# Two small transfers made one, and 68 stores issued by another engine, in an attention and two-layer kernel

## The chip, the cores and the metric

The kernel runs on one core of a Trainium2 chip. A core has TensorE (PE, matmuls into PSUM), VectorE (DVE), ScalarE (ACT), GpSimd (POOL) and SyncE (SP, which here only issues DMA transfers and transposes), each working through its own list of instructions in order. Sixteen DMA engines move the data. The metric is the time on the device in microseconds for one execution.

## The reference

Attention with a learned decay over 4 batches, 8 heads, 576 positions and 64 dimensions, then two feed-forward layers over the 2304 tokens:

```python
cum = np.cumsum(np.log(np.clip(f, 1e-4, 1)), axis=-1)
scores = q @ k.T / sqrt(64) + cum[:, :, :, None] - cum[:, :, None, :]   # causal
x = softmax(scores) @ v                     # -> [2304, 512]
x = leaky_relu(x @ w_in, 0.01) @ w_out      # 512 -> 2048 -> 512
h = x @ w_in2                               # 512 -> 1024
solu = h * softmax(h)
y = ((solu - mean) / sqrt(var + 1e-6) * g_ln) @ w_out2
```

## The kernel before

**Stages.** The 32 heads are worked in 16 pairs. For each pair the rows are cut into blocks of 128, and two passes go over them: pass A does blocks 0 and 1 ("full", `prep_full`), pass B does blocks 2 to 4 (`prep_split`, which splits q and k into a high and a low part). Scores are taken on TensorE, the softmax on VectorE and ScalarE, a DMA transpose (`pt<-hl`) turns the probabilities, TensorE multiplies by v, and the sum is put together in an SBUF tile `xr` (L739, L742). At the end of `pair` the tile is stored to DRAM (`xs_d`, L798), from where `load_x` brings it back, by blocks of 256 tokens, as the first layer's input x, and splits it into a high and a low part. The first layer (`ffn_a`) does 9 of the 16 chunks of the hidden layer for each of 9 token blocks and stores its partial sum y to DRAM (`yp_d`, L908; 4 stores of 128 KB for each block, from tiles that the trace calls `yo` or, in their first home, `sd`). The other 7 chunks and the second layer (`ffn_b`, `layer2`) follow when attention is done, from about 470 us on.

**The decay.** `decay` computes the cumulative sums once and stores them to DRAM as `dr_d`, four rows for each head. `prep_full` appends those rows to the tile of q and k of the two heads as contraction rows 64 to 67: for pairs 4 to 15, each of two heads and each of two column ranges (256 wide) had a transfer of its own. Pairs 0 to 3 have their decay in another way (`qa`).

**Weights.** A weight chunk (512 KB) is loaded to a stage tile (`wst`, three of them, early on), unpacked and split by ScalarE, VectorE and GpSimd (L812, L427, L434, L442). The stage is loaded anew when its last reader is done. The x tiles of the first layer are given out only after all operations on the early stages (`main` in the code), as they lie in the same space.

**Order.** Nothing is issued in the order of the program text. Each operation is put down with an engine (or several to choose from), a cost in nanoseconds, a priority and its dependencies; a planner (`P.run`) plays the whole kernel through when it is built, lets each free engine take its most urgent ready operation, and so writes the order of every engine. On the chip each engine then follows its own list and waits on semaphores. A transfer is put down by `move`, whose costs are 475 ns on SyncE and 1,040 ns on GpSimd; the transfer's bytes occupy one model of the DMA engines. A change of an engine or of a cost can therefore move everything behind it. A store on an engine stands in that engine's list until the data that it stores are there.

```python
QUEUES = ("SP",)
d = {SP: 475.0, ACT: 490.0, POOL: 1040.0}
return flex(engs, [d[e] for e in engs], lambda e: queue[e].dma_start(dst(), src()), prio, dma=nbytes / 360.0, **kw)
```

All transfers were issued by SyncE, since `engs` is `QUEUES` where nothing else is said.

Of the kernel before, what the change touches and what calls it, by code (L numbers as in the profile page):

```python
# [47 lines left out]
LD = 51.31  # L48
# [9 lines left out]
TB = 256  # L58
# [4 lines left out]
KB = CQ + 256  # L63
# [286 lines left out]
def mmr(n):  # L350
    return n / 2.4 + 2.5 if n > 255 else 80.0
# [6 lines left out]
def body(tc, kqa, kq, vt, f, wa, w2i, w2o, gln, out):  # L358
# [3 lines left out]
    PE, ACT, DVE, POOL, SP, CTL = "PE", "ACT", "DVE", "POOL", "SP", "CTL"  # L362
# [6 lines left out]
    def tiles(pool, name, n, shape, dt):  # L369
        return [pool.tile(shape, dt, name=f"{name}{i}") for i in range(n)]  # L370
# [10 lines left out]
    xs_d = tiles(dram, "xs_d", B, [128, KD, S], F32)  # L381
    yp_d = tiles(dram, "yp_d", NB, [128, KD, TB], F32)
    dr_d = dram.tile([2 * NP, 4, KQ], F32, name="dr_d")
# [60 lines left out]
    def flex(engs, durs, emit, prio, **kw):  # L444
        box = []
        o = P.op(tuple(engs) if len(engs) > 1 else engs[0], tuple(durs) if len(engs) > 1 else durs[0],
                 lambda: emit(box[0].eng), prio, **kw)
        box.append(o)
        return o

    def copy_f(o, i, n, prio, engs=(ACT, DVE, POOL), scale=None, psum=False, **kw):
        p = 0 if scale is None else 1
        d = {ACT: act(n, p, psum), DVE: (dve(n) if psum else dve2(n)) + 60 * p, POOL: pool1(n) + 84 * p}
        return flex(engs, [d[e] for e in engs], lambda e: copy_on(e, o(), i(), scale and scale()), prio, **kw)
# [7 lines left out]
    def move(dst, src, nbytes, prio, engs=QUEUES, **kw):  # L462
        d = {SP: 475.0, ACT: 490.0, POOL: 1040.0}
        return flex(engs, [d[e] for e in engs], lambda e: queue[e].dma_start(dst(), src()), prio, dma=nbytes / 360.0, **kw)

    def load(buf, dst, src, nbytes, prio, mode="w", **kw):
        return move(dst, src, nbytes, prio, **{mode: [buf]}, **kw)
# [30 lines left out]
    def row(h, p):  # L498

        return KD * h + p if p < KD else 2 * KD + (NP - KD) * h + p - KD  # L500
# [57 lines left out]
    st, QK, VT, U, QA = {}, {}, {}, {}, {}  # L558
# [7 lines left out]
    def prep_full(p, prio):  # L566


        if p < KD:
            bq = QA[0]  # L570
            QK[p] = [[(bq, p), (bq, "n"), (bq, "c")]] * 2, lambda hd: qa[0:66, hd, p], {0: 256, 1: 384}
            return
        bq = P.buf("raw")
        a = lambda r0, r1: bq.t[r0:r1, 0:1024].rearrange("r (h c) -> r h c", h=2)
        load((bq, 0), lambda: a(0, 64), lambda: kqa[p].rearrange("(h d) c -> d h c", h=2), 64 * 1024 * 4, prio - LD)
        for hd in range(2):
            for c0, k0 in ((0, 0), (256, KB)):
                load((bq, (hd, c0)), lambda hd=hd, c0=c0: a(64, 68)[:, hd, c0:c0 + 256], lambda hd=hd, k0=k0: dr_d[row(hd, p), :, k0:k0 + 256], 4096, prio - LD,
                     deps=st["cols"])
        QK[p] = [[bq]] * 2, lambda hd: a(0, 68)[:, hd], {0: 256, 1: 384}  # L580

    def prep_split(p, prio):
# [106 lines left out]
    def scores(p, unit, hd, prio, full):  # L689

        sts, parts, n, at = P.buf("st"), [], 0, 0
        for j, i in enumerate(unit):
            W = 128 * (i + 1)
            joint = i < 2 and len(unit) > 1
            if i == 1 and joint:
                at = 128
            else:
                ps, at = P.buf("ps_s"), 0
            view = lambda at=at, W=W, ps=ps: ps.t[:, at:at + W]
            key = (ps, j) if joint else ps  # L700
            P.op(PE, 4 * W / 2.4 if full else 2 * mmr(W), lambda Q=QK[p], i=i, W=W, view=view: qk_mm(
                Q, full, i, view(), hd, 0, W, True, True), prio, r=QK[p][0][hd], heat=HEAT if full else 1.0,
                **({"rw": [ps]} if at else {"w": [ps]}))
            parts.append([view, sts, j, W, [(n, n + W, 0, W)], key, i])
            n += 2 * W
        for view, _, j, W, _, key, i in parts:
            P.op(DVE, dve(W) + 130, lambda i=i, j=j, view=view: nc.vector.tensor_tensor_reduce(  # L707
                view(), view(), mask[:, 512 - 128 * i:640], -0.125, 3.0e38, ALU.add, ALU.min, sts.t[:, j:j + 1]),
                prio, w=[(sts, j)], rw=[key])
        parts = [x[:6] for x in parts]  # L710
        pt = softmax(parts, prio)
        return {i: (pt, x[4][0][0] // 128) for i, x in zip(unit, parts)}
# [37 lines left out]
    def pv(p, hd, pts, xr, prio):  # L750
        ps, blocks = P.buf("ps_v"), sorted(pts)
        bufs = {id(b): b for b, _ in pts.values()}

        def pe():
            for i in blocks:
                for j in range(i + 1):
                    for k in range(2):
                        mm(ps.t[:, 128 * i:128 * i + 128], vl(p, hd, j), pts[i][0].t[:, pts[i][1] + k * (i + 1) + j, :],
                           j == 0 and k == 0, j == i and k == 1)

        P.op(PE, sum(2 * (i + 1) * mmh(128) for i in blocks), pe, prio, w=[ps], r=[VT[p]] + list(bufs.values()))
        evac(p, hd, ps, xr, 128 * blocks[0], 128 * (blocks[-1] + 1), 128 * blocks[0], prio)

    def pv4(p, pt, xr, prio):
        ps = P.buf("ps_v")

        def pe():
            for hd in range(2):
                o, c = ps.t[:, 64 * hd:64 * hd + 64], slice(64 * hd, 64 * hd + 64)
                for j in range(4):  # L770
                    for k in range(2):
                        mm(o, vl(p, hd, j), pt.t[:, 4 * k + j, c], j == 0 and k == 0, False)
                mm(o, vl(p, hd, 4), pt.t[:, 8, c], False, True)

        P.op(PE, 18 * mmh(64), pe, prio, w=[ps], r=[VT[p], pt])
        for hd in range(2):
            evac(p, hd, ps, xr, 64 * hd, 64 * hd + 64, 512, prio)

    def pair(p, prio, blocks):
        n0 = len(P.ops)  # L780
        b, kd = divmod(p, KD)
        full = len(blocks) == 2
        (prep_full if full else prep_split)(p, prio)
        if 0 in blocks:
            prep_v(p, prio)
        xr = P.buf("xr")
        k = 0
        for hd in range(2):
            pts = {}
            for unit in UNITS[len(blocks)]:  # L790
                pts.update(scores(p, unit, hd, prio + SM + KSTEP * k, full))
                k += 1
            pv(p, hd, pts, xr, prio + AV)
            if hd == HD4 and 4 in blocks:
                pv4(p, scores4(p, prio + SM + KSTEP * k, full), xr, prio + AV)
                k += 1
        c0, c1 = 128 * blocks[0], min(S, 128 * blocks[-1] + 128)
        o = move(lambda: xs_d[b][:, kd, c0:c1], lambda: xr.t[:, c0:c1], 128 * (c1 - c0) * 4, prio - 400, r=[xr])  # L798
        spills.append((b, c0, c1, o))
        attn_ops.extend(P.ops[n0:])  # L800

# [57 lines left out]
    def y_mms(o, c, d, g, n, first, last):  # L859
        w = WO[c].t  # L860
        wh, wl = (w[:, j, 128 * d:128 * d + 128] for j in range(2))
        gh, gl = (g.t[:, j, 0:n] for j in range(2))
        mm(o, wh, gh, first, False)
        mm(o, wh, gl, False, False)
        mm(o, wl, gh, False, last)
# [23 lines left out]
    YPD, FFNB = {}, {}  # L889

    def ffn_a(blk, prio):
        eprio = prio - EP
        xb = load_x(blk, prio, "x")
        gs = [hidden(c, xb, TB, "ps_f", "g", prio + c, eprio + c) for c in range(FA)]
        YPD[blk] = []
        for d in range(KD):
            ps, yo = P.buf("ps_f"), P.buf("yo")
            for q in range(2):
                cs = range(FA // 2 * q, FA if q else FA // 2)

                def pe(cs=cs, d=d, ps=ps):
                    for c in cs:
                        y_mms(ps.t[:, 0:TB], c, d, gs[c], TB, c == 0, c == FA - 1)

                P.op(PE, 3 * len(cs) * mmr(TB), pe, prio + EPD + d, r=[gs[c] for c in cs] + [WO[c] for c in cs],
                     **({"w": [ps]} if q == 0 else {"rw": [ps]}))
            copy_f(lambda yo=yo: yo.t, lambda ps=ps: ps.t[:, 0:TB], TB, eprio + EPD + d, engs=(ACT, DVE), scale=lambda: WSC * WSC, psum=True, w=[yo], r=[ps])
            YPD[blk].append(move(lambda d=d: yp_d[blk][:, d], lambda yo=yo: yo.t, 128 * TB * 4, prio - 3000, r=[yo]))  # L908

    def ffn_b(tb, prio):  # L910
        eprio, blk = prio - 3000, ORDER[tb]
# [233 lines left out]
```

## Time and profile before

| | |
|---|---|
| runs | 849.77, 846.91, 848.83 us; median 848.83 |
| profiled execution | 848.65 us, span 846.9 us from the first to the last instruction |
| granted TensorE clock, mean | 0.993 |
| TensorE busy | 767.9 us (91% of the span) |
| VectorE, ScalarE, GpSimd busy | 519.4, 490.1, 348.8 us |
| DMA | 108.37 MB, all issued through SyncE's queue but for instructions |

Busy time leaves out instructions that only issue a DMA, so SyncE has none, and a GpSimd that issues a store counts as idle. A wait is put down to the operation that came last. The stretch to 90 us is the start (first pairs, weights), 90 to 392 us is attention mixed with the first layer, 392 to 470 us is the first layer alone, and then come the rest and the second layer.

### The profile page before, as it was taken

How to read it: one execution, taken by the hardware profiler on the slowest of the kernel's cores; microseconds unless marked ns; L12 is line 12 of the kernel's file. 1: busy time of each engine (PE TensorE's matmuls, PEld its weight loads, DVE VectorE, ACT ScalarE, POOL GpSimd, SP SyncE). 2: the span in 40 equal slices, each digit the busy share in tenths (PEclk: the TensorE clock that was granted, in tenths of full speed). 3: DMA queues.
4: the chain of work that ended last, by engine and by line, in shares of the span. 5: the costliest groups of instructions: out<-in, count | busy, mean ns of one | idle time of the engine just before them, and what ended most of it. 6: DMA issues, size and time to landing. Idle time of an engine off the chain costs nothing.

```text
span 846.9 us, 16019 instructions
## 1 busy us (share of the span) xinstructions
PE 767.9 (91%) x5648; PEld 695.5 (82%) x5648; DVE 519.4 (61%) x1350; ACT 490.1 (58%) x1242; POOL 348.8 (41%) x448
## 2 busy tenths in 40 slices
PE   1753798979999999999899998999999999999996
PEld 1432698968998999999899987898889988998885
DVE  5788767888888878884654667334633434253551
ACT  4886768889889889884555543232333243333321
POOL 6648545166618564822610443422332233222321
PEclk9999999989999999999999999999999999999999
DMA  8997457687789677694655643321332131312223
GB/s 230 220 223 245 96 130 151 150 221 154 136 162 216 155 163 151 174 160 148 195 172 177 189 104 104 71 79 16 98 71 68 26 87 38 87 26 63 26 56 82
DMA packets 184402, 108.37 MB, mean 128 GB/s; under 512 B 150033, under 2 KB 167137, under 8 KB 184321
## 3 DMA queue, kind: packets, MB, share of 16 engines
q1 hardware_dynamic: 184320, 107.35, 52.3%
q8 instruction: 44, 0.72, 0.4%
q14 instruction: 38, 0.30, 0.1%
HBM read 57.39 MB, written 14.78 MB: 85 GB/s over the span
## 4 chain that ended last, share of the span: by engine, by line
PE 64%; DMA 10%; DVE 9%; ACT 8%; issue 4%; POOL 3%; SPq 0%; ACTq 0%; DVEq 0%; POOLq 0%
PE ps_f L473 40%; PE ph L473 10%; PE py L473 6%; PE ps_s L473 5%; PE ps_v L473 3%; ACT ps_s L657 2%; DMA raw<-w2o 2%; DMA tr<-hl 2%; DMA raw<-kq 2%; DMA wst<-wa 1%; DMA pt<-hl 1%; ACT hl L427 1%; DVE hl L438 1%; DMA qa<-sd 1%; DVE ps_s L707 1%
## 5 line engine op out<-in xcount | busy, mean ns | idle before, releaser
L473 PE MATMUL ps_f<-x,wi 128*128 128x256 f32 x972 | 131.7, 289 | 1.2 <-POOL x L442 1.1
L473 PE MATMUL ps_f<-g,wo 128*128 128x256 f32 x972 | 126.4, 284 | 2.5 <-DVE g L855 2.5
L473 PEld LDWEIGHTS ps_f<-x,wi 128*128 128x128 f32 x972 | 124.7, 193 | 3.1 <-POOL x L442 1.9
L473 PEld LDWEIGHTS ps_f<-g,wo 128*128 128x128 f32 x972 | 120.8, 188 | 4.0 <-DVE g L855 2.9
L473 PE MATMUL ph<-wi,g 128*128 128x512 f32 x408 | 98.5, 397 | 1.4 <-DVE raw L968 1.4
L473 PE MATMUL ps_f<-x,wib 128*128 128x256 f32 x756 | 97.3, 279 | 1.8 <-DVE g L855 1.7
L438 DVE SCALAR_TENSOR_TENSOR hl<-ps_s,st,hl 128x512 f16<-128x512 f32 (+4 forms) x160 | 82.8, 540 | 19.4 <-ACT hl L427 16.5
L473 PEld LDWEIGHTS ps_f<-x,wib 128*128 128x128 f32 x756 | 91.6, 188 | 2.9 <-DVE g L855 2.8
L473 PEld LDWEIGHTS ph<-wi,g 128*128 128x128 f32 x408 | 75.9, 188 | 19.3 <-DVE raw L968 1.6
L855 DVE TENSOR_TENSOR g<-ps_f,g 128x256 fp32r<-128x256 f32 x144 | 60.3, 420 | 48.1 <-ACT ps_f L854 47.2
L853 ACT ACTIVATE g<-ps_f 128x256 fp32r<-128x256 f32 x144 | 54.8, 380 | 59.3 <-PE ps_f L473 58.1
L657 ACT ACTIVATE ps_s<-ps_s,st 128x512 f32<-128x512 f32 (+4 forms) x160 | 78.6, 491 | 10.1 <-DVE st L707 6.1
L473 PE MATMUL ps_f<-wo,x 128*128 128x512 f32 x348 | 84.0, 396 | 0.0
L427 ACT ACTIVATE hl<-ps_s,st 128x512 f16<-128x512 f32 (+4 forms) x151 | 76.1, 532 | 11.6 <-DMA pt<-hl 4.7
L473 PE MATMUL ps_v<-pt,VT 128*128 128x128 f16 (+1 forms) x928 | 62.3, 220 | 20.0 <-DVE xr L742 9.0
L473 PE MATMUL py<-g,wob 128*128 128x256 f32 x567 | 75.6, 278 | 2.0 <-ACT g L427 2.0
L473 PEld LDWEIGHTS ps_f<-wo,x 128*128 128x128 f32 x348 | 64.8, 188 | 15.1
L473 PE MATMUL ps_s<-kq 128*128 128x512 f32 (+5 forms) x256 | 66.7, 380 | 11.6 <-DVE hl L438 5.5
L442 POOL TENSOR_TENSOR kq<-raw,kq 64x576 fp32r<-64x576 f32 (+1 forms) x53 | 67.9, 1283 | 21.5 <-ACT kq L427 15.2
L473 PEld LDWEIGHTS <-VT 128*128 128x128 f16 x928 | 50.0, 102 | 30.4 <-issue 15.4
L473 PEld LDWEIGHTS py<-g,wob 128*128 128x128 f32 x567 | 71.2, 188 | 4.3 <-ACT g L427 2.3
L707 DVE CUSTOM_DVE_ANT_0 ps_s<-ps_s,mask 128x256 f32<-128x256 f32 (+3 forms) x128 | 62.2, 496 | 5.9 <-PE ps_s L473 4.5
(159 smaller groups left out, 1221.7 us busy)
## 6 DMA issues: line engine op xcount, KB each, us to landing
wst<-wa SPq DMA_DIRECT2D x18, 512.0 KB
sd<-xs_d SPq DMA_DIRECT2D x32, 256.0 KB
raw<-kq SPq DMA_DIRECT2D x16, 480.0 KB
raw<-wa SPq DMA_DIRECT2D x14, 512.0 KB
raw<-yp_d SPq DMA_DIRECT2D x18, 256.0 KB
vr<-vt SPq DMA_DIRECT2D x13, 320.0 KB
raw<-w2i SPq DMA_DIRECT2D x8, 512.0 KB
raw<-w2o SPq DMA_DIRECT2D x8, 512.0 KB
```

Of the source, the lines that this page charges most:

```text
L427: nc.scalar.activation(o, i, CP, scale=1.0 if scale is None else scale)
L438: nc.vector.scalar_tensor_tensor(o, a, scale, b, op0=ALU.mult, op1=ALU.subtract)
L442: (nc.vector if eng == DVE else nc.gpsimd).tensor_tensor(o, a, b, op=ALU.subtract)
L473: nc.tensor.matmul(o, lhsT=l, rhs=r, start=start, stop=stop)
L657: P.op(ACT, act(W, 1, True) + 93, lambda view=view, j=j, k=k: nc.scalar.activation(view(), view(), AF.Exp, bias=sts.t[:, j:j + 1], scale=- ...
L707: P.op(DVE, dve(W) + 130, lambda i=i, j=j, view=view: nc.vector.tensor_tensor_reduce(view(), view(), mask[:, 512 - 128 * i:640], -0.125, 3 ...
L853: P.op(ACT, act(n, 0, True), lambda: nc.scalar.activation(g.t[:, 0, 0:n], h(), AF.Prelu, scale=WSC, alpha=0.01), eprio, w=[(g, 0)], r=[ps])
L855: P.op(DVE, dve(n) + 60, lambda: nc.vector.tensor_tensor(g.t[:, 1, 0:n], h(), g.t[:, 0, 0:n].bitcast(F32), op=ALU.subtract), eprio, w=[(g, ...
```

## The change

The two heads' decay rows of one column range are brought by one transfer, so a pair has two of 8 KB instead of four of 4 KB. The store of x at the end of each pair's pass (32 of them) and the stores of the first layer's partial y (36) are issued by GpSimd.

```diff
-        for hd in range(2):
-            for c0, k0 in ((0, 0), (256, KB)):
-                load((bq, (hd, c0)), lambda hd=hd, c0=c0: a(64, 68)[:, hd, c0:c0 + 256], lambda hd=hd, k0=k0: dr_d[row(hd, p), :, k0:k0 + 256], 4096, prio - LD,
-                     deps=st["cols"])
+        for c0, k0 in ((0, 0), (256, KB)):
+            load((bq, c0 + 1), lambda c0=c0: a(64, 68)[:, :, c0:c0 + 256], lambda k0=k0: dr_d[row(0, p):row(1, p) + 1:row(1, p) - row(0, p), :, k0:k0 + 256].rearrange("h r c -> r h c"),
+                 8192, prio - LD, deps=st["cols"])
...
-        o = move(lambda: xs_d[b][:, kd, c0:c1], lambda: xr.t[:, c0:c1], 128 * (c1 - c0) * 4, prio - 400, r=[xr])
+        o = move(lambda: xs_d[b][:, kd, c0:c1], lambda: xr.t[:, c0:c1], 128 * (c1 - c0) * 4, prio - 400, r=[xr], engs=("POOL",))
...
-            YPD[blk].append(move(lambda d=d: yp_d[blk][:, d], lambda yo=yo: yo.t, 128 * TB * 4, prio - 3000, r=[yo]))
+            YPD[blk].append(move(lambda d=d: yp_d[blk][:, d], lambda yo=yo: yo.t, 128 * TB * 4, prio - 3000, r=[yo], engs=("POOL",)))
```

## Rows read from the trace of the kernel before

**Rows 1.** The page: engines' busy time, and the last chain by engine

```profile
PE 767.9 (91%) x5648; PEld 695.5 (82%) x5648; DVE 519.4 (61%) x1350; ACT 490.1 (58%) x1242; POOL 348.8 (41%) x448
...
PE 64%; DMA 10%; DVE 9%; ACT 8%; issue 4%; POOL 3%; SPq 0%; ACTq 0%; DVEq 0%; POOLq 0%
```

**Rows 2.** Stretches: length; busy PE, PEld, DVE, ACT, POOL; clock, DMA share, GB/s

```profile
0.00:90.00 90.00, 38.56 (x138) 26.31 (x138) 65.94 (x202) 63.38 (x168) 58.05 (x70) 1.00 0.84 224
90.00:392.00 302.00, 288.58 (x2627) 271.37 (x2628) 241.43 (x765) 256.86 (x705) 151.35 (x185) 0.98 0.72 156
0.00:470.00 470.00, 402.81 (x3397) 373.14 (x3398) 347.22 (x1033) 360.74 (x967) 234.07 (x283) 0.99 0.72 174
```

**Rows 3.** SyncE's issues by tile: count, ns min/median/max, first and last start

```profile
L464 SPq DMA_DIRECT2D raw<-dr_d x48: 239/290/483, 20.8 to 250.6; - x48
...
L464 SPq DMA_DIRECT2D xs_d<-xr x32: 319/398/575, 38.6 to 392.2; - x32
...
L464 SPq DMA_DIRECT2D yp_d<-sd x18: 319/363/571, 117.0 to 449.6; - x18
L464 SPq DMA_DIRECT2D yp_d<-yo x18: 319/334/535, 124.9 to 456.1; - x18
```

**Rows 4.** SyncE's timeline: start us, us, line, operation

```profile
45.09 0.53 SPq L464 DMA_DIRECT2D xs_d<-xr  x1
...
47.80 0.98 SPq L464 DMA_DIRECT2D wst<-wa  x2
...
49.59 0.48 SPq L464 DMA_DIRECT2D raw<-dr_d  x1
...
60.60 0.53 SPq L464 DMA_DIRECT2D xs_d<-xr  x1
...
61.66 0.33 SPq L464 DMA_DIRECT2D raw<-dr_d  x1
...
187.03 1.04 SPq L464 DMA_DIRECT2D xs_d<-xr  x2
```

**Rows 5.** The chain that ended last, in order of time: start, us

```profile
45.06 2.70 issue
...
59.11 1.56 issue
```

**Rows 6.** TensorE's timeline; in brackets the idle time before and its releaser

```profile
64.69 2.48 PE L473 MATMUL ps_s<-raw 68*128 68x128 f32 x6 [6.17 <-DMA raw<-dr_d]
...
92.41 2.91 PE L473 MATMUL ps_f<-x,wi 128*128 128x256 f32 x12
...
182.98 0.49 PE L473 MATMUL ps_v<-pt,VT 128*128 128x128 f16 x6 [3.53 <-DVE xr L742]
...
189.55 3.35 PE L473 MATMUL ps_f<-x,wi 128*128 128x256 f32 x11 [1.12 <-POOL x L442]
```

**Rows 7.** Short stretches, columns as in rows 2

```profile
63.00:66.00 3.00, 1.31 (x4) 1.25 (x5) 0.94 (x3) 1.67 (x3) 2.51 (x3) 1.00 1.00 329
66.00:84.00 18.00, 5.94 (x12) 2.92 (x11) 16.94 (x41) 12.28 (x26) 14.20 (x12) 1.00 0.69 244
183.00:195.00 12.00, 9.98 (x50) 7.81 (x49) 10.11 (x36) 11.39 (x33) 9.22 (x12) 0.57 0.70 181
```

**Rows 8.** GpSimd's timeline; in brackets the idle time before and its releaser

```profile
47.80 0.19 POOL L671 TENSOR_SCALAR st<-st 128x2 f32<-128x2 f32 x1 [2.74 <-ACT ps_s L657]
...
60.72 0.19 POOL L671 TENSOR_SCALAR st<-st 128x2 f32<-128x2 f32 x1 [1.61 <-ACT ps_s L657]
...
188.77 2.64 POOL L442 TENSOR_TENSOR x<-sd,x 128x256 fp32r<-128x256 f32 x3
```

**Rows 9.** GpSimd's groups by line: count, busy us, mean ns, idle before

```profile
L442 POOL TENSOR_TENSOR hl<-raw,hl 128x1024 f16<-128x1024 f32 x17 | 36.9, 2169 | 29.0 <-ACT hl L427 29.0
L442 POOL TENSOR_TENSOR x<-sd,x 128x256 fp32r<-128x256 f32 x48 | 35.8, 767 | 6.2 <-ACT x L427 3.1 <-DVE x L430 1.1 <-DVE s L967 0.8
```

**Rows 10.** VectorE's line 671: ns min/median/max, first and last start

```profile
L671 DVE TENSOR_SCALAR st<-st x22: 124/148/1129, 51.3 to 366.4; 128x1 f32<-128x1 f32 x17, 128x2 f32<-128x2 f32 x5
```

## The prediction, made before the change was timed

> **What bounds the kernel now.** I read the page first: which engine is full, and what the chain that ended last consists of. TensorE is busy 91% of the span, and TensorE makes up 64% of that chain; SyncE's own queue is 0% of it [rows 1]. The reader should see there that the queue which the change relieves sets almost nothing directly: rounded to 0%, under half a per cent of 846.9 us, it is at most 4.2 us. The second view is the busy time by stretch. In the first 90 us TensorE works 38.56 us and stands 51.4; from 90 to 392 us (attention mixed with the first layer) it works 288.58 of 302 and stands only 13.4 [rows 2]. So after about 92 us a faster side engine can hardly pay, while each microsecond taken from the start, before the first matmuls of the first layer at 92.41 [rows 6], is a microsecond of the end. In the start no engine is full over the whole 90 us (VectorE 65.94, GpSimd 58.05) [rows 2], so I read it piece by piece: the chain, SyncE's timeline and TensorE's timeline.
>
> What holds the first layer back is in the code: its x tiles are made only when every operation on the early weight stages has been planned and its space released. The weights pass through three stages, each loaded again by SyncE when the last reader is done. The chain goes through two such reloads: GpSimd's last reader ends, and 2.70 and 1.56 us go by until SyncE issues the next weight load or the load behind it [rows 5].
>
> **The change part by part.** Decay rows: 12 pairs had four transfers of 4 KB each, 48 issues at a median of 290 ns; they become 24 of 8 KB. The bytes stay, SyncE loses 24 x 0.290 = 7.0 us of issuing [rows 3]. Stores: 32 of x (median 398 ns), 18 + 18 of y (363 and 334 ns) leave SyncE: 12.7 + 6.5 + 6.0 = 25.3 us [rows 3]. In all 32 us, of which only what lies on the path counts.
>
> On the path I find this. At 45.06 GpSimd frees a stage; SyncE issues an x store at 45.09 for 0.53 us and comes to the weight load only at 47.80. At 59.11 the same: the x store at 60.60 takes 0.53 us ahead of the next load, and one decay row at 61.66 another 0.33 [rows 4, 5]. Taken out: 0.53 + 0.53 + 0.33 = 1.4 us, if nothing else takes the places.
>
> The larger part is a wait. The four decay transfers of the eighth pair are issued from 49.59 to 61.66 us, with transposes and weight loads between them [rows 4], and TensorE stands 6.17 us until the last has landed and the scores begin at 64.69 [rows 6]. Two transfers in place of four complete a pair at its second issue, so I expect this wait mostly to go. It isn't worth 6.17 us: the scores feed VectorE, and what is late next is VectorE's work on the weights. VectorE is busy only 0.94 of 3 us from 63 to 66, and then 16.94 of 18 until 84 [rows 7]. The earlier scores can fill 3 - 0.94 = 2.06 us of idle VectorE; I take three quarters, 1.6 us, since ScalarE and the weights' own waits share that stretch. The bounds are nothing (the weights are not ready sooner) and the whole 6.17.
>
> What is added: 68 issues on GpSimd. The trace has no transfer issued by GpSimd. Its bounds by rows are the shortest compute instruction in front of such a place, 0.19 us [rows 8], and the longest group, 2.169 us [rows 9]; I take 1.0 us, by the operation on a tile of the yp store's size, 0.767 [rows 9], and the 1.04 that the planner is told. That is 68 us on an engine busy 234 of the first 470 us [rows 2]; with the upper bound 147 us, and 381 of 470. Either way it fits. In the start it fits in place: the stores at 45.09 and 60.60 meet a GpSimd that waits 2.74 us until 47.80 and 1.61 us until 60.72 for others [rows 4, 8]. I price it at nothing there; the cover is these waits, and without them each store would cost its 1.0 us. Between 90 and 392 the cover is TensorE's own load.
>
> A port may be a second price. One VectorE instruction of 148 ns median took 1,129 ns [rows 10]. If each store held up one VectorE instruction by as much, 68 x 0.98 = 67 us, counted as if all lay between 90 and 392 us, would meet 302 - 241 = 61 us of idle VectorE [rows 2], and 67 - 61 = 6 us would be lost; I take nothing, since most instances lie near the median. The Trainium skill's SBUF — State Buffer, section "Who interferes with whom", states such a mechanism: GpSimd and some kinds of VectorE instruction exclude each other at a shared port for a whole instruction, and a transfer issued by GpSimd can't have its descriptors written meanwhile. By the rule the sum would be that of rival (c) below. The slow instance agrees with its first half; no row here can show the second.
>
> Moved waits: a store waits for its producer, now in GpSimd's order instead of SyncE's. Behind it on GpSimd stand the splits of q and k and of x, and TensorE waits for those. Behind it on SyncE stood the transposes; they gain what GpSimd's queue loses. I set this at zero, with the bounds of the rivals below.
>
> The order of every engine is planned anew, since the planner counts 475 ns of SyncE less and 1,040 ns of GpSimd more per store. No row prices a new order; the nearest is the worst place of the present one after 92 us. TensorE stands 3.53 us up to 182.98 [rows 6], and from 183 to 195 the granted clock averages 0.57, a mixture of the 1.2 and 2.4 GHz levels, after that idle time: 12 x 0.43 = 5.2 us of full speed lost [rows 7]. Such a place costs 8.7 us; I put the new order between one fewer and one more, and at zero.
>
> Sum: 1.4 + 1.6 = 3.0 us off the profiled execution. That execution took 848.65 us, 1.75 more than its span, and the median of the three runs is 848.83, so no correction: 848.65 - 3.0 = **845.7 us**.
>
> **The rivals.** (a) *Absorbed.* The weights gate the start, not the scores: VectorE, full from 66 to 84, finishes when it did, and only some of the 1.4 us stays: 848 us. For it speaks that VectorE's load is unchanged; against it the 2.06 idle us just ahead.
>
> (b) *GpSimd becomes late: slower.* Two x stores are issued by SyncE together at 187.03 [rows 4]; GpSimd runs the last splits of x from 188.77, and TensorE waits 1.12 us for them at 189.55 [rows 6, 8]. Two stores in front of those splits would put 2 x 1.0 us there, at a block's start and at the lower clock. If the new order does so at one block's start with the idle time and the clock of the present worst place, the price is 8.7 - 3.0 = 5.7 us net, 854 us; without the gain at the start 857. It decides once a store, with its wait, takes over 3.0 us from TensorE in all. Against it: GpSimd has 302 - 151 = 151 idle us in the stretch [rows 2].
>
> (c) *VectorE is held up by the stores: slower.* The 6 us above, with the start's gain kept: 848.65 - 3.0 + 6 = 852 us. For it the one long instance, against it the median [rows 10]. It decides once the stores hold up VectorE by more than its 61 idle us [rows 2].
>
> (d) *The worst place goes too.* With stores off SyncE, the x loads at a block's start come sooner and the stall of 8.7 us at 180 to 195 vanishes: 848.65 - 8.7 = 840 us, or 837 with the start's gain. Against it: that stall hangs on softmax, k and q work as much as on transfers.
>
> (e) *The change doesn't do what it says*: the planner fills SyncE's gaps with earlier weight loads, the transposes land no sooner: as (a).
>
> **How the numbers follow.** Chances: the forecast, 843 to 847 us, 0.40; (a) with (e) 0.25; (b) 0.17; (c) 0.08; (d) 0.10. The bound of 0.3% is 2.5 us on either side of 848.8, which is about what can be told from no change: 846.3 and 851.4. Of the forecast 0.34 lies below it, with (d) that is 0.44 faster; 0.06 of the forecast and 0.21 of (a) give 0.27 the same; (b), (c) and the rest of (a), where the moved stores cost a little, 0.29 slower. The range leaves out half of (d), where it is 837, and that third of (b) that ends at 857: 840 to 856 us. The forecast's own range is 843 to 847.
>
> **What would show it.** Right: the decay transfers of each pair lie side by side on SyncE; no 6 us wait of TensorE for them; the first layer begins near 89.5 instead of 92.4; GpSimd's 68 issues lie in its waits; TensorE's idle time after 90 us stays near 13 us. Wrong: TensorE waiting for x splits or q and k splits of GpSimd behind a store, a granted clock under 1 in another stretch, VectorE's short instructions longer beside stores, or a first layer that begins where it did.

## The result, and the profile after

The changed kernel takes 857.89 us (median of 4 runs, 856.36 to 859.63), the kernel before 847.87 beside it: ratio 1.0122, interval 1.0085 to 1.0158. It is slower by 1.2%, where 845.7 us and a small gain were forecast, and it lies 1.9 us above the range. The profiled execution took 859.63 us, its span 857.4 us, 10.5 more than before.

The page of the changed kernel, engines and GpSimd's new queue, and the shares of its last chain:

```profile
PE 774.0 (90%) x5648; PEld 699.2 (82%) x5648; DVE 539.4 (63%) x1370; ACT 492.0 (57%) x1255; POOL 363.8 (42%) x482
...
q0 software_dynamic: 3264, 9.44, 3.2%
...
PE 50%; DMA 5%; DVE 4%; issue 4%; ACT 2%; POOL 2%; SPq 0%; POOLq 0%; DVEq 0%; ACTq 0%
```

9.44 MB now go through a queue of GpSimd's own. The issues count as GpSimd's busy time, not as idle time as I wrote of the profile before: with the same other operations and 68 stores (experiment 2) GpSimd is busy 386.3 us instead of 348.8. VectorE is busy 20 us longer than in [rows 1]. The chain's shares add up to only 67%, so it wasn't followed over the whole span and I don't compare it.

**The start came out in its times, but not by the forecast way.** SyncE's timeline of the changed kernel, the eighth pair's decay rows:

```profile
48.97 0.28 SPq L464 DMA_DIRECT2D raw<-dr_d  x1
...
50.88 0.34 SPq L464 DMA_DIRECT2D wst<-wa  x1
51.27 0.32 SPq L464 DMA_DIRECT2D raw<-dr_d  x1
```

The pair is complete at 51.27 us instead of 61.66 [rows 4], the 6.17 us wait for it [rows 6] is gone, and the first layer begins at 89.59 us instead of 92.41 [rows 6]. But TensorE then stands 6.08 us for VectorE's splits of q and k (`kq`), and the next pass's scores begin at 69.37 us, where they began at 69.73 before. TensorE's timeline of the changed kernel: these scores, the first matmul of the first layer, and then the end of attention (behind each line the idle time ahead of it):

```profile
69.37 2.79 PE L473 MATMUL ps_s<-kq 128*128 128x512 f32 x6 [6.08 <-DVE kq L442]
...
89.59 0.58 PE L473 MATMUL ps_f<-x,wi 128*128 128x256 f32 x1 [2.67 <-POOL x L434]
...
404.11 0.95 PE L473 MATMUL ps_v<-pt,VT 128*128 128x128 f16 x14
404.87 2.03 PE L473 MATMUL ps_f<-g,wo 128*128 128x256 f32 x15
409.58 0.38 PE L473 MATMUL ps_f<-x,wi 128*128 128x256 f32 x1 [2.68 <-ACT x L427]
413.19 6.89 PE L473 MATMUL ps_f<-x,wi 128*128 128x256 f32 x35 [3.23 <-POOL x L442]
```

**The end of attention is worse.** The same scores and the end of attention before:

```profile
69.73 0.79 PE L473 MATMUL ps_s<-kq 128*128 128x512 f32 x1 [2.56 <-ACT kq L427]
...
390.15 0.95 PE L473 MATMUL ps_v<-pt,VT 128*128 128x128 f16 x14
390.91 10.32 PE L473 MATMUL ps_f<-g,wo 128*128 128x256 f32 x84
401.07 13.12 PE L473 MATMUL ps_f<-x,wi 128*128 128x256 f32 x108
416.52 7.70 PE L473 MATMUL ps_f<-g,wo 128*128 128x256 f32 x62 [2.33 <-DVE g L855]
```

Before, attention's last matmuls (`ps_v`) are followed by 84 + 108 matmuls of the first layer without a gap; in their shadow the last x is stored, loaded and split. After, attention ends 14 us later, only 15 matmuls stand ready behind it, and TensorE waits 2.68 and 3.23 us for splits of x.

By stretches (length, busy PE, PEld, DVE, ACT, POOL, granted clock, DMA share, GB/s), first before (0 to 90 is in [rows 2]):

```profile
90.00:200.00 110.00, 99.49 (x846) 92.59 (x847) 83.42 (x271) 89.23 (x240) 54.19 (x65) 0.95 0.65 149
200.00:392.00 192.00, 189.08 (x1783) 178.78 (x1783) 158.01 (x495) 167.62 (x466) 97.16 (x121) 1.00 0.75 160
392.00:430.00 38.00, 35.67 (x297) 35.46 (x297) 18.77 (x30) 18.32 (x45) 17.68 (x22) 1.00 0.65 202
...
480.00:520.00 40.00, 35.79 (x248) 32.52 (x247) 28.89 (x52) 19.47 (x42) 20.24 (x25) 1.00 0.48 132
```

and after:

```profile
0.00:90.00 90.00, 41.88 (x145) 27.81 (x145) 73.28 (x217) 66.97 (x177) 61.35 (x78) 1.00 0.84 229
...
90.00:200.00 110.00, 99.31 (x835) 92.52 (x835) 80.95 (x258) 84.57 (x234) 56.38 (x71) 0.94 0.64 147
200.00:392.00 192.00, 183.95 (x1707) 173.56 (x1707) 166.72 (x495) 166.51 (x466) 97.30 (x123) 1.00 0.73 154
392.00:430.00 38.00, 30.74 (x263) 29.74 (x262) 16.68 (x36) 18.70 (x47) 17.53 (x26) 0.91 0.61 167
413.00:417.00 4.00, 3.81 (x18) 3.82 (x19) 0.91 (x2) 1.58 (x2) 2.23 (x4) 0.50 0.74 214
...
480.00:520.00 40.00, 39.01 (x287) 36.46 (x286) 28.99 (x49) 19.98 (x42) 16.98 (x22) 1.00 0.46 152
```

Length less busy PE is TensorE's idle time; length times what the clock lacks to 1.00 is what its lower level (1.2 of 2.4 GHz) cost. A mean of 0.91 is a mixture of the two. From 413 to 417 us, right behind the two waits for x, the granted clock is 0.50, the lower level all through. From before to after the idle time changes by 48.1 - 51.4 = -3.3 us (0 to 90), 10.7 - 10.5 = +0.2 (to 200), 8.1 - 2.9 = +5.1 (to 392), 7.3 - 2.3 = +4.9 (to 430), 1.0 - 4.2 = -3.2 (480 to 520); the clock costs 110 x 0.01 = 1.1 us and 38 x 0.09 = 3.4 us more. That is +8.2 us of the 10.5. The start has less idle time (experiments 5 and 6 say what that comes from); the loss lies between 200 and 430 us.

**The stores.** GpSimd's stores in the changed kernel (count, ns min/median/max, first and last start), from the view of the line that issues them:

```profile
L464 POOL DMA_DIRECT2D xs_d<-xr x32: 539/587/768, 37.5 to 406.4; - x32
...
L464 POOL DMA_DIRECT2D yp_d<-sd x18: 539/564/590, 117.4 to 464.8; - x18
L464 POOL DMA_DIRECT2D yp_d<-yo x18: 539/558/590, 125.1 to 471.3; - x18
...
  ACT sd L427: 22.0, 12
  DVE xr L741: 17.7, 11
  ACT yo L427: 14.3, 9
```

A store costs GpSimd 0.56 to 0.59 us, not 1.0. It also stands and waits: the last three lines are GpSimd's idle time ahead of the issues, by what it waited for. The last x store is issued at 406.4 us instead of 392.2 [rows 3].

### The profile page after: what moved, and what is told of

Same layout as the page of the kernel before. It is cut to its first block, busy times and chain, and to the rows that moved or that the text cites. A ratio compares the mean times of both kernels' runs of the same rounds, so it can differ in the third digit from the quotient of the medians.

```text
span 857.4 us, 16054 instructions
## 1 busy us (share of the span) xinstructions
PE 774.0 (90%) x5648; PEld 699.2 (82%) x5648; DVE 539.4 (63%) x1370; ACT 492.0 (57%) x1255; POOL 363.8 (42%) x482
## 3 DMA queue, kind: packets, MB, share of 16 engines
q0 software_dynamic: 3264, 9.44, 3.2%
## 4 chain that ended last, share of the span: by engine, by line
PE 50%; DMA 5%; DVE 4%; issue 4%; ACT 2%; POOL 2%; SPq 0%; POOLq 0%; DVEq 0%; ACTq 0%
PE ps_f L473 30%; PE ph L473 10%; PE py L473 7%; PE ps_s L473 2%; DMA tr<-hl 2%; PE ps_v L473 1%; DMA sd<-xs_d 1%; DMA pt<-hl 1%; DVE hl L438 1%; DMA raw<-w2o 0%; DMA raw<-wa 0%; DVE g L442 0%; SPq L464 0%; ACT hl L427 0%; DVE g L854 0%
## 5 line engine op out<-in xcount | busy, mean ns | idle before, releaser
L473 PE MATMUL ps_f<-x,wi 128*128 128x256 f32 x972 | 135.9, 295 | 10.7 <-POOL x L442 3.9
L473 PEld LDWEIGHTS ps_f<-x,wi 128*128 128x128 f32 x972 | 128.5, 199 | 12.9 <-POOL x L442 4.4
L427 ACT ACTIVATE hl<-ps_s,st 128x512 f16<-128x512 f32 (+4 forms) x150 | 75.4, 533 | 14.5 <-DVE st L674 4.4
L473 PEld LDWEIGHTS ps_s<-kq 128*128 128x128 f32 (+1 forms) x256 | 43.1, 202 | 30.0 <-DVE hl L438 14.6
```

The source lines that it names most:

```text
L427: nc.scalar.activation(o, i, CP, scale=1.0 if scale is None else scale)
L473: nc.tensor.matmul(o, lhsT=l, rhs=r, start=start, stop=stop)
```

## The experiments

Five theories came out of this. **Order**: the planner wrote another order for every engine, and that alone is slower. **Queue**: GpSimd stands behind its stores and is late with its splits. **Port**: the stores hold up VectorE. **Constant**: the planner is told 1,040 ns for a store that takes 590, and gives GpSimd's work away. **Tail**: the x rows for the last blocks land too late at the end of attention. All experiments were timed beside the kernel before; its medians there are 846.5 to 847.6 us.

**1. The decay rows in one transfer, stores on SyncE.** The first hunk of the diff alone.

> The decay rows merged, all stores still issued by SyncE. Theory A (the loss comes with the stores: the planner, told 1,040 ns for each, moves GpSimd's splits to VectorE and attention ends later): near the kernel before, 845 to 849 us. Rival M (the merged transfers alone reorder everything): 854 us or more.

856.13 us, ratio 1.0125 (1.0097 to 1.0153). With no store on GpSimd the kernel is as slow as with all 68. Queue, port and constant can't be the cause here.

**2. The stores on GpSimd, the order of before.** The planner still counts a store as SyncE's; only the instruction goes out on GpSimd, at the same place among the others. TensorE's, VectorE's and ScalarE's lists are those of before.

```diff
-    def move(dst, src, nbytes, prio, engs=QUEUES, **kw):
+    def move(dst, src, nbytes, prio, engs=QUEUES, via=None, **kw):
...
-        return flex(engs, [d[e] for e in engs], lambda e: queue[e].dma_start(dst(), src()), prio, dma=nbytes / 360.0, **kw)
+        return flex(engs, [d[e] for e in engs], lambda e: queue[via or e].dma_start(dst(), src()), prio, dma=nbytes / 360.0, **kw)
...
-        o = move(lambda: xs_d[b][:, kd, c0:c1], lambda: xr.t[:, c0:c1], 128 * (c1 - c0) * 4, prio - 400, r=[xr])
+        o = move(lambda: xs_d[b][:, kd, c0:c1], lambda: xr.t[:, c0:c1], 128 * (c1 - c0) * 4, prio - 400, r=[xr], via=POOL)
...
-            YPD[blk].append(move(lambda d=d: yp_d[blk][:, d], lambda yo=yo: yo.t, 128 * TB * 4, prio - 3000, r=[yo]))
+            YPD[blk].append(move(lambda d=d: yp_d[blk][:, d], lambda yo=yo: yo.t, 128 * TB * 4, prio - 3000, r=[yo], via=POOL))
```

> The kernel before, its plan untouched (all orders of PE, DVE and ACT as before), but the 68 stores are put into GpSimd's list at the place in the plan where SyncE had them. Theory A (the loss is in the plan): 845 to 850 us. Rival Q (the loss is on the chip: GpSimd stands in front of stores, about 80 us of idle time in the changed kernel, and the splits behind come late): 854 to 862 us. Rival P (stores hold up VectorE at a shared port): VectorE's busy time grows by 15 us or more with the same instructions.

850.68 us, ratio 1.0048 (1.0027 to 1.0069): the stores cost some 4 us of themselves. The stretches of this kernel:

```profile
90.00:200.00 110.00, 98.37 (x831) 91.13 (x832) 82.61 (x264) 87.63 (x236) 61.52 (x81) 0.94 0.64 148
200.00:392.00 192.00, 185.74 (x1743) 176.25 (x1741) 159.61 (x497) 168.53 (x467) 117.54 (x155) 1.00 0.74 161
392.00:430.00 38.00, 36.86 (x328) 36.55 (x327) 19.07 (x30) 17.28 (x44) 21.55 (x29) 1.00 0.59 188
```

TensorE's idle time from 200 to 392 us is 6.3 us instead of 2.9. That fits the queue theory, at a smaller size, but its path isn't traced: TensorE waits there mostly for VectorE (`vs` 2.2 us, `hl` 1.4) and for transposes (1.9), and only 0.4 us for GpSimd itself. VectorE is busy 82.61 and 159.61 us beside the stores, 83.42 and 158.01 without them; over the whole execution it is 521.8 us instead of 519.4, far from the 15 us of the port theory. And from 392 to 430 us nothing is lost.

**3. The order of the changed kernel, stores issued by SyncE.** The mirror image: the planner counts the stores as GpSimd's, the chip issues them on SyncE (`via=SP`).

> The changed kernel, its plan untouched (planner still counts 1,040 ns of GpSimd for a store), but on the chip SyncE issues the stores. Theory A: as slow as the changed kernel, 855 to 860 us, attention ending (last store of x) near 404 us. Rival Q: back to 845 to 849 us.

857.8 us, ratio 1.0133 (1.011 to 1.0157), the changed kernel's time to within the interval. Its stretches:

```profile
200.00:392.00 192.00, 185.29 (x1730) 175.25 (x1729) 165.17 (x505) 167.81 (x469) 79.75 (x94) 1.00 0.72 155
392.00:430.00 38.00, 30.92 (x262) 29.87 (x260) 17.51 (x31) 19.16 (x46) 16.12 (x19) 0.91 0.61 175
```

Relieved of every store, GpSimd has 18 us less to do from 200 to 392, and the hole from 392 to 430 is the same (7.1 us, clock 0.91). TensorE's idle time from 200 to 392 us stays at 6.7 us too. Experiments 2 and 3 hold one thing fixed each, and most of the loss goes with the order.

**4. The changed kernel with the right constant.** `POOL: 1040.0` becomes `590.0`.

> The changed kernel with one number of the planner corrected: 590 ns for a transfer on GpSimd, as the trace of the changed kernel measured (median 587 for x, 564 and 558 for y), in place of 1,040. Theory A: part of the loss goes, 846 to 853 us, with fewer splits of q, k and x on VectorE. Rival Q: still 855 to 860 us. If the order alone is a lottery, anything from 843 to 860.

855.05 us, ratio 1.0098 (1.0075 to 1.0121). It is about 3 us faster than the changed kernel, near what the intervals can tell; as it is one more new order, that can't be put down to the constant, and the rest stays.

**5 and 6. The merged transfer, and the whole change, in the order of before.** The planner counts four decay transfers as it did; the chip issues the merged one at the first head's place and nothing at the second's. Experiment 6 adds experiment 2's stores.

```diff
+        both = lambda c0, k0: queue[SP].dma_start(
+            a(64, 68)[:, :, c0:c0 + 256], dr_d[row(0, p):row(1, p) + 1:row(1, p) - row(0, p), :, k0:k0 + 256].rearrange("h r c -> r h c"))
...
-                load((bq, (hd, c0)), lambda hd=hd, c0=c0: a(64, 68)[:, hd, c0:c0 + 256], lambda hd=hd, k0=k0: dr_d[row(hd, p), :, k0:k0 + 256], 4096, prio - LD,
-                     deps=st["cols"])
+                flex(QUEUES, [475.0], lambda e, hd=hd, c0=c0, k0=k0: None if hd else both(c0, k0), prio - LD, dma=4096 / 360.0,
+                     w=[(bq, (hd, c0))], deps=st["cols"])
```

> The decay rows merged on the chip, while the planner still counts four transfers, so that every engine keeps the order of the kernel before. Theory L (what costs time is that the order is planned anew, whatever the reason): 843 to 848 us, the 6 us wait of TensorE for decay rows near 60 us shorter, VectorE not idle there. Rival M (merged transfers themselves cost time): 853 us or more, as in the run with the merge alone.

845.98 us, ratio 0.9996 (0.9976 to 1.0017): nothing. In TensorE's timeline of this kernel the wait for decay rows is gone, and a wait of 8.98 us for ScalarE's splits of q and k stands in place of the 6.17 and 2.56 us of the kernel before. The end of attention is as before:

```profile
67.47 0.80 PE L473 MATMUL ps_s<-kq 128*128 128x512 f32 x1 [8.98 <-ACT kq L427]
...
90.16 2.05 PE L473 MATMUL ps_f<-x,wi 128*128 128x256 f32 x8
...
387.93 0.95 PE L473 MATMUL ps_v<-pt,VT 128*128 128x128 f16 x14
388.70 10.32 PE L473 MATMUL ps_f<-g,wo 128*128 128x256 f32 x84
398.85 13.12 PE L473 MATMUL ps_f<-x,wi 128*128 128x256 f32 x108
```

The first layer begins at 90.16 us, but that isn't the merged transfer's doing: experiment 10 below has the start of the kernel before, with four transfers, and its first layer begins at 90.60.

```profile
90.60 2.91 PE L473 MATMUL ps_f<-x,wi 128*128 128x256 f32 x12
```

In the order of before TensorE stands 51.1 to 51.4 us of the first 90 with four transfers (before, experiments 2, 10 and 15) and 51.0 and 51.3 with the merged one (5 and 6). So the changed kernel's 48.1 us come with its new order, and not from the merged transfer alone.

> The whole change on the chip (rows merged, 68 stores issued by GpSimd) in the order of the kernel before. Theory L: the same as the stores alone in that order (850.7) or a little better, 846 to 851 us. Rival Q or M: 855 to 860 us, as the changed kernel.

848.79 us, ratio 1.0036 (1.0012 to 1.006). So the change itself costs about 3 us of the 10 (1 to 5 by the interval).

**7, 8 and 12. A new order and nothing else.** The kernel before, with one constant of the planner off by a hair: a transfer on SyncE (7), an operation with two inputs on GpSimd (8), an operation on VectorE (12); the diff shows the three one after the other. The work stays the same; only its order can change, and which engine does an operation that several may do.

```diff
-        d = {SP: 475.0, ACT: 490.0, POOL: 1040.0}
+        d = {SP: 474.0, ACT: 490.0, POOL: 1040.0}
...
 def pool2(n):
-    return 2.104 * n + 148
+    return 2.104 * n + 147
...
 def dve(n):
-    return 1.042 * n + 70
+    return 1.042 * n + 70.5
```

> The kernel before, with nothing changed on the chip's side but the order: the planner is told 474 ns in place of 475 for a transfer on SyncE, which reorders every engine. Theory L (the constants of the planner are fitted to the one order of the kernel before): 852 to 858 us, with a hole of TensorE between 392 and 430 us as in the changed kernel. Rival S (it is the stores or the merge that make the worse order): 844 to 850 us.

> As the run before it, another irrelevant number: the planner is told 1 ns less for a subtraction on GpSimd (147 in place of 148). Theory L: 850 to 858 us. Rival S: 844 to 850 us.

> The kernel before with a third irrelevant nudge: the planner is told 0.5 ns more for every full-rate instruction on VectorE. Theory L: 850 to 862 us. If two nudges out of two were slow by accident, 844 to 850 us.

861.57, 859.43 and 860.17 us, ratios 1.0185 (1.0146 to 1.0223), 1.0168 (1.0131 to 1.0204) and 1.0165 (1.0138 to 1.0193). Half a nanosecond in a table costs as much as the change under study, or more. TensorE's timeline of experiment 7 has the same hole:

```profile
405.04 0.95 PE L473 MATMUL ps_v<-pt,VT 128*128 128x128 f16 x14
405.81 3.47 PE L473 MATMUL ps_f<-g,wo 128*128 128x256 f32 x27
410.71 0.38 PE L473 MATMUL ps_f<-x,wi 128*128 128x256 f32 x1 [1.44 <-ACT x L427]
413.74 6.65 PE L473 MATMUL ps_f<-x,wi 128*128 128x256 f32 x35 [2.65 <-POOL x L442]
```

**11. The same nudge on the changed kernel** (experiment 8's line).

> The changed kernel with the irrelevant nudge that the kernel before has had: 147 in place of 148 ns for a subtraction on GpSimd in the planner. Theory L (a new order costs what it costs, with or without the change): 853 to 861 us, not clearly other than the kernel before with the same nudge (859.4). Rival S (the change makes orders worse): above 862.

856.63 us, ratio 1.0117 (1.0095 to 1.014): the changed kernel, planned once more, stays where it was.

**9 and 10. The tail's data early.** The x blocks 7 and 8 read the first batch's rows of x, which are long in DRAM, in the changed kernel (9) and in the kernel before (10).

```diff
-                     lambda q=q, b=b, s=s, n=n: xs_d[b][:, 2 * q:2 * q + 2, s:s + n], 128 * 2 * n * 4, prio - 4000, deps=deps)
+                     lambda q=q, b=0 if tag == "x" and blk > 6 else b, s=s, n=n: xs_d[b][:, 2 * q:2 * q + 2, s:s + n], 128 * 2 * n * 4, prio - 4000, deps=deps)
```

> The changed kernel in its own order, but the first layer's last two token blocks read batch 0's rows of x, stored long before, instead of the rows that the last pairs of heads store (so the values of those blocks are other ones); the work is the same. Theory H (most of the loss is one place: after the last pair, TensorE has too little first-layer work in front of it to cover storing, loading and splitting x): TensorE's 2.7 and 3.2 us waits for x and the low clock between 405 and 420 us go, 848 to 852 us. Rival D (the loss is spread over the whole stretch with attention): 855 to 858 us.

> The same edit on the kernel before, as a control (values of those two blocks are other ones). Theory H: there the place costs almost nothing, so 844 to 847.5 us. Rival D: the same.

859.13 us, ratio 1.0153 (1.0127 to 1.0179), and 846.1 us, 0.9996 (0.9976 to 1.0016). The tail theory falls: the data are there and the waits stay at 2.68 and 3.02 us. What stands ahead of the splits is in ScalarE's timeline of experiment 9:

```profile
404.78 0.66 ACT L427 ACTIVATE wib<-raw 128x512 fp32r<-128x512 f32 x1 [1.24 <-DMA xs_d<-xr]
405.35 1.01 ACT L427 ACTIVATE x<-sd 128x256 fp32r<-128x256 f32 x3
```

The splits of x stand in line behind a weight split (`wib`), whose tile is free only when the last x store has landed.

**13, 14 and 15. The x splits ahead of those weight splits**, in experiment 9's kernel (13), in the changed kernel (14) and in the kernel before (15). Only the emission is changed: `wib` and `wob` operations that fall among block 7's x splits are held until the splits are out.

```diff
-                    o.emit()
+                    if self.xops and (o.eng != "PE" and o.dma is None and any(b.tag.name in ("wib", "wob") for b in o.bufs)
+                                      or any(b.t is x.t for h in self.held for x in h.bufs for b in o.bufs)):
+                        self.held.append(o)
+                    else:
+                        o.emit()
...
+                if tag == "x" and blk == 7:
+                    P.xops.extend(P.ops[n0:])
```

> The changed kernel with batch 0's rows read for the last two token blocks (their values are other ones), and five instructions moved: the first two pieces of work on the next weights, whose tiles lie in attention's space and so wait until the last store of x has landed, go behind the splits of x on ScalarE, GpSimd and VectorE. Every other order stays. Theory W (those weights stand in front of x in the lists, which is why reading stored rows alone gave nothing): 852 to 855.5 us, the 2.7 and 3.0 us waits of TensorE before x shorter by 3 us or more together, the clock nearer 1. Rival D (the loss is spread; the hole only moves): 857 to 860 us.

> The changed kernel with its own rows of x and only those five instructions moved. Theory W: a little, 855.5 to 857.5 us, since x itself must still be stored and loaded first. Rival D: 857 to 859 us.

> The kernel before with the same five instructions moved. There TensorE has 192 matmuls of the first layer in front of it at that place, so both theories: 845 to 848 us; as a version to keep it would need under 844.

860.16 us (1.0152, 1.0136 to 1.0168), 862.31 us (1.0179, 1.0159 to 1.0198) and 851.02 us (1.0035, 1.0018 to 1.0053). No gain anywhere. TensorE's timeline of experiment 13 shows why:

```profile
401.85 2.03 PE L484 MATMUL ps_f<-g,wo 128*128 128x256 f32 x15
404.66 0.38 PE L484 MATMUL ps_f<-x,wi 128*128 128x256 f32 x1 [0.78 <-ACT x L438]
407.63 5.70 PE L484 MATMUL ps_f<-x,wi 128*128 128x256 f32 x35 [2.59 <-POOL x L453]
419.41 1.86 PE L484 MATMUL ps_f<-x,wi 128*128 128x256 f32 x7 [6.08 <-DVE g L865]
```

The waits for x shrink from 2.68 + 3.02 to 0.78 + 2.59 us, and 6.08 us for VectorE's `g` come in their place. VectorE now stands behind weights that are still being loaded, as the timelines of ScalarE (first line) and VectorE show:

```profile
410.40 0.80 ACT L438 ACTIVATE wk<-raw 128x512 f16<-128x512 bf16 x1 [4.19 <-DMA raw<-wa]
...
411.23 0.69 DVE L822 SCALAR_TENSOR_TENSOR raw<-raw,wk 128x512 int32<-128x512 int32 x1 [4.24 <-ACT wk L438]
```

The hole moves; it wasn't filled by mending the wait that ends last.

## Why the prediction was wrong

**The step that failed** is the one on the new order: "Such a place costs 8.7 us; I put the new order between one fewer and one more, and at zero." Seven orders were planned here that differ from that of before (the changed kernel's, which experiment 3 shares, and those of experiments 1, 4, 7, 8, 11 and 12): all end 0.98% to 1.85% above it, none below. The size is 8 to 16 us, one to two such places; the error was to set it even on both sides and so at zero. The order of before is the best of those seen, so a new one was likelier to lose than to gain. Why it is the best (constants chosen by trying, say) no run shows.

**The start** is a second step that failed, hidden by times that came near the forecast: the decay transfers 2.3 us apart, their wait gone, the first layer at 89.59 us where 89.5 was forecast, 3.3 us less idle by 90 us. The 1.6 us rested on "The earlier scores can fill 3 - 0.94 = 2.06 us of idle VectorE". The runs show the next gate instead: TensorE waits for the splits of q and k, in the changed kernel until 69.37 us (before 69.73), and with the order held 8.98 us in one piece in place of 6.17 + 2.56. That is nearer to rival (a), with q and k in the weights' place. The 1.4 us of SyncE's places show nowhere either: with the stores off SyncE in the old order (experiment 2) the first layer begins at 91.57 us, and three executions with an unchanged start begin it at 90.60 to 92.76 (before, 10, 15). The 3.3 us came with the new order; that they came near my 3.0 is luck. Whether a microsecond taken from the start is one of the end, as I wrote, no run shows, since with the order held none clearly took one.

**The stores** were priced at 1.0 us each and nothing on the path. The first was too high, 0.56 to 0.59 us measured, inside the bounds; the second too low: in the old order they cost 846.85 x 0.0048 = 4.1 us (2.3 to 5.8), most of it in TensorE's waits between 200 and 392 us. My cover, TensorE's own load, didn't hold there. That the stores' waits on GpSimd are what reaches TensorE is likely, not traced.

**Rival (b)** names nearly the time that came, 854 to 857 us, and wrongly explains it: with SyncE issuing the stores in the same order the kernel is as slow (experiment 3). What the stores themselves cost is the 4 us in the old order.

**Rival (c)**, VectorE held up by the stores, isn't seen. GpSimd's other operations seem to do it: the two slow instances of the line of [rows 10] (1.13 us up to 52.42 and 0.99 us up to 73.32) each end 0.03 us after an operation of GpSimd that began before them (ends at 52.39 and 73.29). The issue of a store does not: in experiment 2, 83 instructions of VectorE overlap an issue and nothing else on GpSimd, and they take 24 ns in the mean, and 94 at most, over the shortest of their kind in the kernel before; the 523 that overlap nothing on GpSimd also take 24 in the mean. In the old order VectorE's busy time is 521.8 and 522.3 us with the stores (2 and 6) against 517.2 to 520.1 without (before, 5, 10, 15), a few us and not 67. The rule of the Trainium skill (SBUF — State Buffer, "Who interferes with whom"), by which GpSimd's descriptors would wait for some of VectorE's instructions, should show in the issues' own length, or in their landing. No issue takes over 0.768 us; they land in 2.5 us (x) and 2.9 us (y) in the median, 7.3 at most. That one maximum could be such a case; nothing here separates it. Of the 20 us that VectorE works longer in the changed kernel, 14.5 are there without the stores too (experiment 3, 533.9 us): the planner gave it splits that GpSimd had. VectorE's group of splits of q and k, 0 to 480 us, before:

```profile
L442 DVE TENSOR_TENSOR kq<-raw,kq 64x384 fp32r<-64x384 f32 (+1 forms) x11 | 12.8, 1160 | 0.3
```

and after:

```profile
L442 DVE TENSOR_TENSOR kq<-raw,kq 64x384 fp32r<-64x384 f32 (+1 forms) x22 | 23.6, 1072 | 0.6
```

**Rival (d)** didn't come: from 90 to 200 us idle time and clock stayed nearly as they were (10.7 us after 10.5, 0.94 after 0.95). **Rival (a)**: with the order held the merge was indeed absorbed, 845.98 us, and 846.52 for the kernel before beside it. **Rival (e)** wasn't looked into beyond the eighth pair, which was complete 10 us earlier.

**Open.** That the new order costs the time is shown; what in it does is shown only in part. Every kernel in the old order (before, 2, 5, 6, 10) has 84 + 108 matmuls behind the end of attention, each of the seven new orders has 15 to 54 and then a wait. A late end of attention isn't what they share: in experiments 1 and 8 it ends only 2 and 3 us later than before. And the hole is only a part: from 200 to 392 us the kernels in a new order with all stores on SyncE (1, 3, 7, 8, 12) have 5.2 to 8.7 us of TensorE's idle time, those in the old order 2.1 to 2.9 (before, 5, 10, 15); no experiment looked into that. Whether the hole's root is that small stock, the place of the weight splits or the loads behind them, experiments 9 to 15 did not settle. No version beat both kernels; the best, experiment 5, can't be told from the kernel before.

## What to carry to other kernels

Where a planner writes the order, a small edit is two changes: itself, and a new order of everything. Price the second from nudges that change nothing else (three here cost 1.65 to 1.85%), and measure the first with the order held, by sending an instruction out on another engine at its old place. An edit that is worth less than the spread over orders can't be judged from one new order; tuning the planner's constants again on both sides would be the way, and wasn't tried here. And follow a wait that is gone to the next one: a stage that begins earlier in one execution may do so in another without the edit.

## What the hardware showed that I hadn't expected

A store of 128 to 160 KB issued by GpSimd occupies it for only 0.54 to 0.77 us, not much more than the 0.32 to 0.58 us that SyncE takes for it [rows 3]; and VectorE's instructions beside such an issue are no longer than beside an idle GpSimd (experiment 2). GpSimd spends far more in front of the stores than on them: 54 us in the three largest groups of waits shown above, though how much of that it would have been idle anyway isn't separated.
